# The down product of two FFN tiles by seven products instead of eight

## The chip, the cores and the metric

The kernel runs on one core of a Trainium2 chip. Four engines matter: TensorE (in the profile PE, its weight loads PEld), VectorE (DVE), ScalarE (ACT) and GpSimd (POOL); transfers are issued by SyncE (SP). The metric is the device time of one execution in microseconds, smaller is better. The kernel before was timed three times: 2411.37, 2413.34 and 2414.25 us, median 2413.34.

## The reference

A transformer block in fp32 over x of 2048 rows and 576 columns: attention with 32 heads of 18 that share one key and one value head, then a gated FFN without nonlinearity and with 4608 hidden columns. Cut to what matters here:

```python
h  = x + attention(layernorm(x))
n  = layernorm(h)
g  = n @ w_gate          # (2048, 576) @ (576, 4608)
u  = n @ w_up
h2 = h + (g * u) @ w_down   # (2048, 4608) @ (4608, 576): the down product
```

## The kernel before, in words

Rows are handled in four blocks b of 512 (TB). To keep fp32 accuracy with the faster fp32r matmuls, each operand is split into a high part (a cast to fp32r) and a low part (the rest, a subtraction on VectorE); a product is then three matmuls: high by high, high by low, low by high. `split` does the two steps. During the FFN the cast (`self.cast`) is on ScalarE for activations, on GpSimd for weights.

Attention of a block runs in pairs: `pair` issues the scores of two heads (two matmuls into one of two PSUM buffers named s) and the exp on ScalarE (P<-s); `flush` issues the matmuls of P by the values (acc). Attention of later blocks is woven into the FFN of an earlier block: `ffn(b)` issues one pair at every fourth step as long as `self.more(b + 2)` holds.

`ffn(b)` loops over 36 tiles f of 128 hidden columns. A tile has 27 steps of two matmuls, one for the gate (pg) and one for up (pu). Beside attention pg and pu lie in the two banks of tag f; without attention they are the halves of one of the two s buffers (gu). After the steps: `act.copy(g, pg)`, hf = pu * g on VectorE, the split of hf (ha, hl), the values of the pending pairs, and one piece of other work (`run_aux`: normalising heads, transposing a chunk, the output projection yo of the next block).

The down product is issued once per three tiles (CF = 3), after the first tile of the next three: eight groups (four row groups by two column halves of 288), each of nine matmuls (three tiles by three parts) into one PSUM bank, and an addition of the bank to h on VectorE. Banks go round over three, two of tag f and one of tag m (`ps_y`). In the loop:

```python
if k == 0 and todo:
    drain(self.down(b, *todo))
```

Weights come by DMA: `load_w` (wr, gate and up of one tile) and `load_wd` (wdr, one tile of w_down). `split_w` casts and splits the next tile's gate and up weights at step 3 (ws); `split_wd` does the same for w_down at steps 12 and 15 (wds). At a block's end the transposes of the normalised rows of the next block (`spread`, tx, X) alternate with the groups of the last down product.

The order on each engine is written by hand: it is the order in which the Python code issues instructions (`manual_schedule`). Tiles bring the semaphores for true dependences and for the reuse of buffers. A later instruction on an engine does not pass an earlier one.

The chunks of attention output go through oT, a buffer of nine times 512 columns; `transposed`, `chunk_of` and `project` use it.

## Time and profile before

| what | value |
|---|---|
| median of three runs | 2413.34 us |
| the profiled execution | 2414.04 us |
| its span, first to last instruction | 2412.3 us |
| granted TensorE clock, mean | 0.993 |
| TensorE busy | 2357.6 us, 98% |
| VectorE busy | 999.1 us, 41% |
| ScalarE busy | 1235.2 us, 51% |
| GpSimd busy | 357.9 us, 15% |

A row of the page or of an answer names line, engine, operation and tile (out<-in), then shape and count. In groups there follow the busy time, the mean of one in ns, the idle time ahead of it and what ended that; in a timeline a row begins with start and length in us, and the bracket at the end has the idle time before and its cause; the chain of waits in order of time has start, length and what was at work. Rows by tile give least, middle and greatest length in ns. Stretches (from:to) have length, TensorE's busy time, the granted clock PEclk, the share of the DMA engines and GB/s.

### The profile page before, as it was taken

What the parts mean: (1) busy time and instruction counts of PE and PEld (TensorE: products, weight loads), DVE (VectorE), ACT (ScalarE), POOL (GpSimd) and SP (SyncE); (2) the same over time, 40 slices, a digit from 0 to 9 for tenths busy, and PEclk for the clock granted to TensorE, in tenths of its full rate; (3) what the DMA queues carried; (4) which work ended last, traced back from release to release, by engine and by line L of the source; (5) the groups of instructions that cost most, each with busy time, mean ns of one, the idle gap of its engine ahead of it and who ended that gap; (6) DMA issues with size and microseconds to landing.
All of it is one profiled execution on the core that took longest, in us unless ns stands there. A gap on an engine that the chain in (4) does not pass through costs nothing.

```text
span 2412.3 us, 44160 instructions
## 1 busy us (share of the span) xinstructions
PE 2357.6 (98%) x18833; PEld 1658.7 (69%) x18833; DVE 999.1 (41%) x1719; ACT 1235.2 (51%) x1381; POOL 357.9 (15%) x406
## 2 busy tenths in 40 slices
PE   5999989999999999999999999999999999999999
PEld 4434434676776677777766767776777688888888
DVE  7323334343333345333333344433333364555454
ACT  4877867656555655555565556456555501111111
POOL 3000000111111111111111111111111112222221
PEclk9999999999999999999999999999999999999999
DMA  4212231222122221521222122322212222422321
GB/s 138 85 60 73 69 105 44 73 77 76 59 67 68 72 63 63 151 67 45 77 68 68 59 76 67 112 95 73 69 58 65 65 70 98 144 95 98 99 89 60
DMA packets 69298, 190.54 MB, mean 79 GB/s; under 512 B 8328, under 2 KB 9096, under 8 KB 69096
## 3 DMA queue, kind: packets, MB, share of 16 engines
q1 hardware_dynamic: 69096, 187.66, 24.6%
q8 instruction: 149, 2.44, 0.4%
q14 instruction: 53, 0.43, 0.1%
HBM read 159.39 MB, written 19.40 MB: 74 GB/s over the span
## 4 chain that ended last, share of the span: by engine, by line
PE 95%; DVE 2%; ACT 1%; issue 1%; DMA 1%; POOL 0%; SPq 0%; ACTq 0%; POOLq 0%; DVEq 0%
PE acc L503 19%; PE y L712 19%; PE pg L739 14%; PE gu L739 12%; PE s L498 12%; PE pu L739 11%; PE yo L608 3%; PE psq L335 2%; PE pt L541 1%; ACT P L499 1%; PE to L134 0%; PE tx L657 0%; DVE bsa L100 0%; PE psr L335 0%; DVE XT L86 0%
## 5 line engine op out<-in xcount | busy, mean ns | idle before, releaser
L499 ACT ACTIVATE P<-s 128x1024 f32<-128x1024 f32 x1024 | 1035.6, 1026 | 683.6 <-PE s L498 583.4
L739 PE MATMUL pg<-X,ws 64*128 64x512 f32 x2565 | 706.1, 392 | 0.0
L739 PE MATMUL pu<-X,ws 64*128 64x512 f32 x2565 | 705.7, 392 | 0.0
L739 PEld LDWEIGHTS pg<-X,ws 64*128 64x128 f32 x2565 | 474.4, 186 | 65.5 <-issue 6.1
L739 PEld LDWEIGHTS pu<-X,ws 64*128 64x128 f32 x2565 | 474.0, 186 | 40.3
L503 PE MATMUL acc<-P,V 128*32 128x512 f32 x4096 | 491.2, 599 | 2.6 <-DVE os L514 2.0
L712 PE MATMUL y<-wds,ha 128*128 128x288 f32 x2304 | 464.1, 296 | 2.5 <-ACT ha L85 1.2
L498 PE MATMUL s<-q,kT 56*128 56x512 f32 x2048 | 434.0, 421 | 12.9 <-DVEq L388 8.0
L712 PEld LDWEIGHTS y<-wds,ha 128*128 128x128 f32 x2304 | 368.4, 188 | 27.8 <-issue 25.2
L712 PE MATMUL y<-wds,hl 128*128 128x288 f32 x1152 | 340.0, 295 | 0.1
L498 PEld LDWEIGHTS s<-q,kT 56*128 56x128 f32 x2048 | 193.4, 185 | 208.3 <-ACT P L499 101.9
L85 POOL CAST ws<-wr 128x1152 fp32r<-128x1152 f32 x144 | 165.9, 1152 | 974.2 <-PE pu L739 414.2
L739 PE MATMUL gu<-X,ws 64*128 64x512 f32 x2646 | 307.2, 389 | 0.0
L503 PEld LDWEIGHTS acc<-P,V 128*32 128x32 f32 x4096 | 114.4, 109 | 250.4 <-issue 225.1
L739 PEld LDWEIGHTS gu<-X,ws 64*128 64x128 f32 x2646 | 247.3, 185 | 55.2 <-issue 4.2
L758 DVE TENSOR_TENSOR hf<-pu,g 128x512 f32<-128x512 f32 x95 | 65.7, 691 | 528.6 <-ACT g L754 528.6
L714 DVE TENSOR_TENSOR h<-h,y 128x288 f32<-128x288 f32 x384 | 172.7, 453 | 253.4 <-PE y L712 253.2
L754 ACT COPY g<-gu 128x512 f32<-128x512 f32 x49 | 28.8, 587 | 377.7 <-PE gu L739 377.7
L85 POOL CAST wds<-wdr 128x576 fp32r<-128x576 f32 x144 | 146.1, 1033 | 488.0 <-PE y L712 481.3
L712 PEld LDWEIGHTS y<-wds,hl 128*128 128x128 f32 x1152 | 216.1, 188 | 0.4 <-DVE hl L86 0.4
L86 DVE TENSOR_TENSOR ws<-wr,ws 128x1152 fp32r<-128x1152 f32 x144 | 204.4, 1420 | 0.0
L86 DVE TENSOR_TENSOR hl<-hf,ha 128x512 fp32r<-128x512 f32 x144 | 100.6, 699 | 151.3 <-ACT ha L85 151.3
(145 smaller groups left out, 1309.3 us busy)
## 6 DMA issues: line engine op xcount, KB each, us to landing
wr<-in_wgu_dram SPq DMA_DIRECT2D x144, 576.0 KB
wdr<-in_wd_dram SPq DMA_DIRECT2D x144, 288.0 KB
q<-q_dram SPq DMA_DIRECT2D x64, 216.0 KB
q_dram<-qs SPq DMA_DIRECT2D x16, 504.0 KB
X<-X SPq DMA_DIRECT2D x28, 256.0 KB
x<-in_x_dram SPq DMA_DIRECT2D x16, 288.0 KB
h<-in_x_dram SPq DMA_DIRECT2D x16, 288.0 KB
out_dram<-h SPq DMA_DIRECT2D x16, 288.0 KB
```

Of the source, the lines that this page charges most:

```text
L85: (copy or self.cast)(hi, src)
L86: self.dve.tensor_tensor(lo, src, f32(hi), ALU.subtract)
L335: pe.matmul(ps[:r], w[o:o + 64], m[o:o + 64], start=(k == 0), stop=(k == 13))
L498: self.pe.matmul(s_[:, i], self.kT[o:o + 56, t * P:(t + 1) * P], q[o:o + 56, pr], start=True, stop=True)
L499: self.act.activation(p_, s_, AF.Exp, scale=SCALE)
L503: self.pe.matmul(acc[32 * j:32 * j + 32, :], self.V[:, t, :], Ps[j // 2][:, j % 2, :], start=(t == 0), stop=(t == NT - 1), skip_group_chec ...
L608: pe.matmul(y[:, :HD], m, k, start=(i == 0), stop=(i == len(ms) - 1))
L712: pe.matmul(y[:, :HD], m, w, start=(i == 0), stop=(i == len(ms) - 1))
L714: dve.tensor_tensor(hs, hs, y[:, :HD], ALU.add)
L739: pe.matmul(ps, w[o:o + 64, wk, c], X[o:o + 64, xk, c], start=(j == 0), stop=(j == 26))
L754: act.copy(g, pg)
L758: dve.tensor_tensor(hf, pu, g, ALU.mult)
```

## The change

The down product is issued per pair of tiles. The left matrix (512 rows by 256 hidden columns) is seen as two by two blocks of 256 by 128, the right one (256 by 576) as two by two blocks of 128 by 288. Strassen's method in Winograd's form gives the four result blocks from seven products instead of eight, with four sums S of left blocks and four sums T of right blocks. Each product is three matmuls as before, for each of two row groups of 128: 14 stages of three matmuls per pair of tiles.

- `left`, after each odd tile: casts and subtractions for the plain left blocks that take part as they are (256 and 512 elements), the four sums S on VectorE, then the cast of S (1024 elements, ScalarE) and its subtraction. The tiles ha, hl go; A holds all parts.
- `sums_wd` and `split_wd`, at step 5 of each odd tile, on GpSimd: four sums T of 288 elements, then casts of 288, 576 and 1152.
- `rest_wd`, at step 12 of the next even tile, on VectorE: the three subtractions, and after them the loads of two further tiles of w_down.
- `down` runs the 14 stages over three banks in turn. A bank is read after each product and the next product is added to it in place, without starting at zero, so one product enters several results. Nine of the fourteen reads are additions on VectorE; five are copies on ScalarE into a small buffer (`tmp`), from which GpSimd adds to h.
- Place: after the even tile's steps, without attention ahead of that tile's g, with attention after its hf and the values.
- At a block's end `rest_wd` runs at step 18 of the last tile, ahead of `normal`.
- Room for A is taken from oT after block 0; attention output of later blocks goes through a buffer of one chunk (o_hl), and the fifth chunk is transposed after the fourth is projected. The buffer for raw wo goes from two to one.

```diff
-CF = 3
-NC = NF // CF
+NC = NF // 2
+HT = TB // 2
...
+    def sums_wd(self, n):
+
+        (b11, b12), (b21, b22) = (halves(self.wdr[i], HD) for i in (n, n + 1))
+        T = self.T
+        for i, (x, y) in enumerate(((b12, b11), (b22, T[:, 0]), (b22, b12), (b21, T[:, 1]))):
+            self.nc.gpsimd.tensor_tensor(T[:, i], x, y, ALU.subtract)
+
+    def wd_parts(self, n):
+        w = self.wds
+        return ((w[:, :, 0], self.wdr[n][:, 0:HD]), (w[:, :, 1:3], self.wdr[n + 1].rearrange("p (a d) -> p a d", a=2)),
+                (w[:, :, 3:7], self.T))
+
     def split_wd(self, n):
...
+        self.wds = self.wp.tile([P, 2, 7, HD], F32R, tag="wds", bufs=1, name=f"wds{n}")
+        for w, src in self.wd_parts(n):
+            self.nc.gpsimd.tensor_copy(w[:, 0], src)
+
+    def rest_wd(self, n):
+
+        for w, src in self.wd_parts(n):
+            self.dve.tensor_tensor(w[:, 1], src, f32(w[:, 0]), ALU.subtract)
+        for i in (n, n + 1):
+            del self.wdr[i]
+            self.load_wd(i + 2)
+
+    def left(self, hf):
+
+        dve, S, A = self.dve, self.S, self.A
+        (a11, a21), (a12, a22) = (halves(x, HT) for x in hf)
+        self.split(A[:, 0, 0], A[:, 1, 0], a11)
+        self.split(A[:, 0, 1:3], A[:, 1, 1:3], hf[1].rearrange("p (a q) -> p a q", a=2))
+        dve.tensor_tensor(S[:, 0], a21, a22, ALU.add)
+        dve.tensor_tensor(S[:, 1], S[:, 0], a11, ALU.subtract)
+        dve.tensor_tensor(S[:, 2], a11, a21, ALU.subtract)
+        dve.tensor_tensor(S[:, 3], a12, S[:, 1], ALU.subtract)
+        self.split(A[:, 0, 3:7], A[:, 1, 3:7], S)
+
+    def down(self, b, pair, W):
+
+        pe, dve, act, sp, pool = self.pe, self.dve, self.act, self.sp, self.nc.gpsimd
         h = self.h[b]
...
+        banks = [self.ps_f(f"y{b}_{pair}_0"), self.ps_f(f"y{b}_{pair}_1"), self.ps_m(f"y{b}_{pair}_2")]
+        for i, (t, bank, (x, w), first, (s, n), on_dve) in enumerate(STAGES):
+            y = banks[bank]
+            x_, w_ = ([o[:, k, j] for k in range(2)] for o, j in ((self.A, x), (W, w)))
+            ms = [(x_[k], w_[l]) for k, l in ((0, 0), (0, 1), (1, 0))]
+            for j, (m, k) in enumerate(ms):
+                pe.matmul(y[:, :HD], m[:, t * P:(t + 1) * P], k, start=(first and j == 0), stop=(j == 2), skip_group_check=True)
+            hs = h[:, t + 2 * s, n * HD:(n + 1) * HD]
+            if on_dve:
                 dve.tensor_tensor(hs, hs, y[:, :HD], ALU.add)
...
+            else:
+                z = self.tmp[:, self.n_tmp % 5]
+                self.n_tmp += 1
+                act.copy(z, y[:, :HD])
+                pool.tensor_tensor(hs, hs, z, ALU.add)
+            yield
+        if pair == NC - 1:
+            for s in (1, 3, 0, 2):
                 sp.dma_start(self.out[b * TB + s * P: b * TB + (s + 1) * P, :], h[:, s, :])
...
-                    if j == 12 and k == 1:
+                    if j == 5 and k:
+                        self.sums_wd(n_ - 1)
                         self.split_wd(n_ - 1)
-                    if j == 15 and k:
-                        self.split_wd(n_)
+                    if j == 12 and k == 0 and f:
+                        self.rest_wd(n_ - 2)
+                    if j == 18 and f == NF - 1:
+                        self.rest_wd(n_ - 1)
...
+            if todo and not on:
+                drain(self.down(b, *todo))
             g = self.hh.tile([P, TB], F32, tag="g", bufs=1, name=f"g{n_}")
             act.copy(g, pg)
...
-            self.split(a, l, hf)
-            hid.append((a, l))
+            hid.append(hf)
+            if k:
+                self.left(hid)
+                hid = []
             self.flush(len(self.pend))
+            if todo and on:
+                drain(self.down(b, *todo))
             if f < NF - 1:
                 self.run_aux()
...
+            todo = (f // 2, self.wds) if k else None
...
+P1, P2, P3, P4, P5, P6, P7 = (0, 0), (1, 1), (6, 2), (2, 6), (3, 3), (4, 4), (5, 5)
+
+
+STAGES = [(0, 0, P1, True, (0, 0), True), (1, 1, P1, True, (0, 0), True), (0, 2, P5, True, (1, 1), False),
+          (0, 0, P6, False, (0, 1), True), (1, 1, P6, False, (0, 1), False), (0, 2, P3, False, (0, 1), True),
+          (0, 0, P7, False, (1, 1), False), (1, 1, P7, False, (1, 1), True), (1, 2, P5, True, (1, 1), True),
+          (0, 0, P4, False, (1, 0), True), (1, 1, P4, False, (1, 0), False), (1, 2, P3, False, (0, 1), False),
+          (0, 0, P2, True, (0, 0), True), (1, 1, P2, True, (0, 0), True)]
```

A stage names the row group, the bank (0 and 1 of tag f, 2 of tag m), the pair of left and right parts, whether the bank starts at zero, the block of h, and whether VectorE reads.

More of the change, by code (lines that the diff above doesn't have):

```diff
@@ L532, in normalise @@
         del self.os[g]
-        for c in (g // 2,) * (g % 2) + (4,) * (g == NG - 1):
+        for c in (g // 2,) * (g % 2) + (4,) * (b == 0 and g == NG - 1):
             self.aux.append((self.round, lambda c=c: self.chunk(b, c), None))
@@ L614, in project @@
                     self.fill(2.4)
+        if c == 3 and b:
+            self.aux.append((self.round, lambda: self.chunk(b, 4), None))
         if c == 4:
@@ L690, in load_wd @@
             self.sp.dma_start(r, self.wd[n % NF])
-    def split_wd(self, n):
-        k = n % CF
-        if k == 0:
-            self.wds = self.wp.tile([P, 2, CF, D], F32R, tag="wds", bufs=1, name=f"wds{n}")
-        self.split(self.wds[:, 0, k], self.wds[:, 1, k], self.wdr.pop(n), self.nc.gpsimd.tensor_copy)
-        self.load_wd(n + 2)
-    def down(self, b, chunk, parts, wds):
-        pe, dve, sp = self.pe, self.dve, self.sp
-        h = self.h[b]
-        for s in range(NQ):
-            for n in range(2):
-                y = self.ps_y(2 * s + n, f"y{b}_{chunk}_{s}_{n}")
-                ms = []
-                for k, (a, l) in enumerate(parts):
-                    wh, wl = wds[:, 0, k, n * HD:(n + 1) * HD], wds[:, 1, k, n * HD:(n + 1) * HD]
-                    a_, l_ = a[:, s * P:(s + 1) * P], l[:, s * P:(s + 1) * P]
-                    ms += [(a_, wh), (a_, wl), (l_, wh)]
-                for i, (m, w) in enumerate(ms):
-                    pe.matmul(y[:, :HD], m, w, start=(i == 0), stop=(i == len(ms) - 1))
-                hs = h[:, s, n * HD:(n + 1) * HD]
-                dve.tensor_tensor(hs, hs, y[:, :HD], ALU.add)
-                yield
-            if chunk == NC - 1:
-                sp.dma_start(self.out[b * TB + s * P: b * TB + (s + 1) * P, :], h[:, s, :])
@@ L723, in ffn @@
             n_ = NF * b + f
-            k = f % CF
+            k = f % 2
             w = self.ws.pop(n_)
@@ L876, in run @@
             self.flush(len(self.pend))
+            del self.oT
+            self.room()
             for b in range(NB):
@@ L890, in both, with halves @@
         live = [x for x in live if next(x, drain) is not drain]
+def halves(ap, n):
+    return ap[:, 0:n], ap[:, n:2 * n]
 def f32(ap):
```

39 lines of the change are left out of this document (22 added, 17 removed).

## The prediction

> **What bounds the kernel now.** I read the page's totals and chain first, then the chain of waits over the last fifth in order of time, then timelines around single tiles. Lines of the page:
>
> ```profile
> span 2412.3 us, 44160 instructions
> PE 2357.6 (98%) x18833; PEld 1658.7 (69%) x18833; DVE 999.1 (41%) x1719; ACT 1235.2 (51%) x1381; POOL 357.9 (15%) x406
> ...
> PE 95%; DVE 2%; ACT 1%; issue 1%; DMA 1%; POOL 0%; SPq 0%; ACTq 0%; POOLq 0%; DVEq 0%
> ...
> L754 ACT COPY g<-gu 128x512 f32<-128x512 f32 x49 | 28.8, 587 | 377.7 <-PE gu L739 377.7
> ```
>
> TensorE carries 95% of the chain, so what it issues counts in full, and so does every wait put in front of it. The last row counts 49 FFN tiles whose sums lie in gu (no attention beside them); the other 95 of 144 have attention. With 36 tiles in each of four blocks, attention ends at tile 22 of block 2. Of the 72 new pair products, 45 then run beside attention (17, 17 and 11 in blocks 0, 1, 2), 23 without (6 and 17 in blocks 2, 3), three at block ends and one at the kernel's end.
>
> Rows of the chain of waits in order of time (start, us):
>
> ```profile
> 900.93 9.53 PE y L712 x72
> ...
> 2205.13 9.72 PE y L712 x72
> 2214.84 18.59 PE gu L739 x162
> ...
> 2384.68 12.49 PE gu L739 x108
> ...
> 2397.25 0.60 ACT g L754
> ...
> 2397.87 0.70 DVE hf L758
> ...
> 2398.60 0.63 ACT ha L85
> ...
> 2399.25 0.70 DVE hl L86
> ...
> 2408.77 0.46 DVE h L714
> ```
>
> One tile's gate and up take 18.59/3 = 6.20 us. Seventy-two down matmuls take 9.72 us, and 9.53 where they follow a projection's matmuls: 9.53/72 = 0.1323 each, and 0.19 to start. The rows from 2397.17 (2384.68 + 12.49) on show the chain that stands behind the last tile and is hidden behind others: g, product hf, cast, subtraction, 2.8 us until 2399.95.
>
> **The change part by part.**
>
> Matmuls. Per pair 14 x 3 = 42 replace 48; over 72 pairs 432 go: 432 x 0.1323 = -57.2 us. Products start 72 times for 48: 24 x 0.19 = +4.6.
>
> Reads. 14 rather than 5.3 a pair, over three banks in turn. The output projection already does this with groups of three matmuls and every read on VectorE (timeline):
>
> ```profile
> 1299.27 3.49 PE L608 MATMUL yo<-wos,oT 128*128 128x288 f32 x24
> 1299.97 3.29 DVE L609 TENSOR_TENSOR h<-h,yo 128x288 f32<-128x288 f32 x8 [0.85 <-PE yo L608]
> ```
>
> A group takes 3.49/8 = 0.44 us, a read 3.29/8 = 0.41. A stage of 0.397 us may wait for the read three stages back, which has 0.79 us; only nine of fourteen reads are VectorE's. I cost it at nothing (upper end 14 x (0.44 - 0.397) x 72 = +43). At the end of a product beside attention pu takes the bank of stage 13 and waits some 0.1 us: +4.5.
>
> What must stand before a product. This decides. `left` puts on VectorE, after each odd tile, four sums of 256 elements and subtractions of 256, 512 and 1024, and on ScalarE casts of the same sizes, the last of which needs all four sums. `rest_wd` puts subtractions of 288, 576 and 1152 behind them, after the subtraction for the next tile's gate and up weights. Product stage 2 needs the S of `left` and the T of `rest_wd`. Durations:
>
> ```profile
> L86 DVE TENSOR_TENSOR ws<-wr,ws x144: 1345/1353/1816, 406.9 to 2385.1; 128x1152 fp32r<-128x1152 f32 x144
> ...
> L85 POOL CAST wds<-wdr x144: 667/669/1796, 431.5 to 2390.7; 128x576 fp32r<-128x576 f32 x144
> L86 DVE TENSOR_TENSOR wds<-wdr,wds x144: 742/751/1215, 435.1 to 2393.7; 128x576 fp32r<-128x576 f32 x144
> ...
> L664 DVE TENSOR_TENSOR X<-tx,X 128x1024 fp32r<-128x1024 f32 x7 | 8.5, 1219 | 4.3 <-ACT X L666 4.3
> L666 ACT CAST X<-tx 128x1024 fp32r<-128x1024 f32 x7 | 6.8, 1026 | 0.3 <-PE tx L657 0.3
> L309 POOL TENSOR_TENSOR wq_l<-wqr,wq_h 128x630 fp32r<-128x630 f32 x3 | 4.5, 1504 | 0.2
> L309 POOL TENSOR_TENSOR wq_l<-wqr,wq_h 128x360 fp32r<-128x360 f32 x1 | 0.9, 879 | 0.1
> ```
>
> Between 576 and 1152 elements VectorE takes (1353-751)/576 = 1.045 ns an element, so 256 take 0.43 us and 288 0.45. ScalarE's 0.63 for 512 and 1.03 for 1024 give 0.43 for 256. GpSimd takes 2.3 ns an element between 360 and 630, so 288 take 0.71.
>
> Tiles without attention. Count from the end of an odd tile's gate and up matmuls. Product hf ends at 1.40 (rows at 2397); the cast of 512 at 2.06, its subtraction at 2.78 (the 256 piece, from the first tile, fits in that wait); four sums, 4.50; cast of 1024, 5.57; its subtraction, 6.83; weights 1152, 8.18; `rest_wd` 0.45 + 0.75 + 1.35, 10.73. TensorE has the next tile's 6.20 and stages 0 and 1 (0.79) to fill this: it arrives at 6.99. With the handover 10.8 is the lower end. GpSimd is still casting while VectorE forms the sums, and the two slow each other:
>
> ```profile
> 2214.91 2.40 POOL L85 CAST wds<-wdr 128x576 fp32r<-128x576 f32 x2 [8.56 <-PE y L712]
> 2215.25 1.53 DVE L86 TENSOR_TENSOR ws<-wr,ws 128x1152 fp32r<-128x1152 f32 x1
> 2216.71 1.88 DVE L86 TENSOR_TENSOR wds<-wdr,wds 128x576 fp32r<-128x576 f32 x2
> ```
>
> Two casts of 0.67 take 2.40; VectorE takes 1.53 + 1.88 for 1.35 + 1.50, 0.56 more. After a product GpSimd has a cast 1.15, sums 4 x 0.71, casts of 2016 elements some 2.3 and the next cast 1.15: about 7.5 us behind its last add, so 1 to 2 us of it meet the sums. I take 11.0, upper end 11.7. Stall 11.0 - 6.99 = 4.0; 23 x 4.0 = +92 (87 to 108). The down product's own cover is gone: before, it stood between a tile's chain and the next wait. The five adds (3.6 us) lie beside the product; the next weight cast behind them ends some 2 us into a tile of 6.20.
>
> The Trainium skill (SBUF — State Buffer, Who interferes with whom) says that VectorE with two SBUF inputs and a GpSimd read lock each other out, the later one for the whole instruction. The three rows agree in kind (2.40 for 1.34). By the full lock the stall would be some 2 us longer, +46 on the sum.
>
> The clock. Stretches of 3.41 us (us, PE busy, PEclk, DMA):
>
> ```profile
> 35.51:38.93 3.42, 2.15 (x10) 1.00 0.64 208
> ...
> 49.17:52.58 3.41, 0.46 (x2) 1.00 0.33 80
> 52.58:55.99 3.41, 2.25 (x14) 0.50 0.90 324
> ...
> 329.06:332.47 3.41, 1.48 (x12) 1.00 0.36 118
> 332.47:335.89 3.42, 0.00 (x0) 1.00 0.76 198
> ...
> 2407.78:2411.19 3.41, 0.96 (x8) 1.00 0.42 167
> 2411.00:2411.50 0.50, 0.00 (x0) 0.69 0.00 0
> ```
>
> After stretches with 0.46, 0.00 and 0.96 us of TensorE work the clock is half; after 1.48 and 2.15 it is not. The new gap is about 4.8 us with 0.8 us of work in it, so some stretches fall to 0.8 to 1.0. By where they can begin I estimate half of the pairs, each with one stretch or a little more at half speed, 1.9 us: 23 x 0.5 x 1.9 = +22 (0 to 23 x 3.4 = 78). The Trainium skill (TensorE: Matmul & The Clock Gate, What's actually happening) asks for a whole idle window of 3.4 us; the gap never has one, so by it this term is zero and the sum 22 less. The row at 2407.78 disagrees, with 0.96 us of work, so I keep the term.
>
> Tiles beside attention. Timeline there:
>
> ```profile
> 1503.91 1.02 ACT L499 ACTIVATE P<-s 128x1024 f32<-128x1024 f32 x1 [0.43 <-PE acc L503]
> ...
> 1504.83 0.61 ACT L85 CAST ha<-hf 128x512 fp32r<-128x512 f32 x1
> ...
> 1505.47 0.69 DVE L86 TENSOR_TENSOR hl<-hf,ha 128x512 fp32r<-128x512 f32 x1 [1.26 <-ACT ha L85]
> ...
> 1506.92 2.19 ACT L499 ACTIVATE P<-s 128x1024 f32<-128x1024 f32 x2 [1.49 <-PE s L498]
> ...
> 1507.37 0.19 PEld L498 LDWEIGHTS s<-q,kT 56*128 56x128 f32 x2
> ...
> 1508.53 0.19 PEld L498 LDWEIGHTS s<-q,kT 56*128 56x128 f32 x2
> ```
>
> Every answer of the trace shows ScalarE in the order of its queue, and there the cast of S now stands ahead of the next tile's exps: exp ends 1504.93, cast 256 1505.3, cast 512 1505.9, subtraction 1506.6, four sums 1508.2, cast of S 1509.3, first exp 1510.3. The third scores (1508.53) need the buffer that this exp empties: stall 1.8 us. ScalarE then keeps pace (1.02 an exp, scores each 1.16, from 1507.37 to 1508.53). `rest_wd`, 2.6 us after S, is no matter here: behind it lie most of a tile with scores and its values. In five cases, by the order in which the changed program issues, a projection (yo) follows an odd tile: its fourth group, due at 1507.5, needs a VectorE read that queues behind the subtraction of S (1510.5): some 3.4. Together 40 x 1.8 + 5 x 3.4 = +89 (0 to 100).
>
> Block ends and the last pair. Between a block's last tile and the next block's first, 13.0 us pass now (2067.12 - 2041.64 - 12.54):
>
> ```profile
> 2041.64 12.54 PE L739 MATMUL gu<-X,ws 64*128 64x512 f32 x108
> ...
> 2067.12 3.25 PE L739 MATMUL gu<-X,ws 64*128 64x512 f32 x26
> ```
>
> After, `rest_wd` of the last pair waits on GpSimd (adds until 0.8 us after the previous product, then 1.15 + 2.84 + 2.33: 7.1) and stands ahead of the normalisation (2.04) and of hf on VectorE: hf ends near 11.2, S near 16.6, twelve stages with X's subtractions between them near 24.4, so 18.2 after the tile's matmuls. With the 30 matmuls' 3.97 counted above: 3 x (5.2 + 3.97) = +27.6 (10 to 40). The end goes likewise from 15.1 (2412.3 - 2397.17) to some 19.3 us: without the normalisation hf ends near 9.1 and S near 14.5 after the previous product, twelve stages 19.3, so 13.1 behind the tile, then the read 0.46, the output 3.1 as now, and 2.6 because all four row blocks go out behind the last read: 4.2 + 3.97 = +8.2.
>
> Sum: -57.2 + 4.6 + 4.5 + 92 + 22 + 89 + 27.6 + 8.2 = +190.7. The profiled execution took 2414.04, 1.7 more than its span and 0.7 more than the median of the three; 2413.34 + 190.7 = 2604.
>
> **The rivals.**
>
> Faster: the matmuls removed are all that counts, because no chain ends last. -57.2 + 4.6 + 4.5 = -48, 2365 us. For it: 95% TensorE, 41% VectorE. Against it: the chain 10.8 must fall under 6.99. It decides only if the sums, casts and subtractions overlapped, and each needs the one before it. Chance 0.06.
>
> Attention hides its stall, because scores or values already issued cover the late exps: only +102, 2515. For it: ScalarE is 51% busy. Against: TensorE issues in order, and two s buffers are all. Chance 0.11.
>
> Sharing and clock worse: the full lock (+46) or most pairs at half clock (+30 or more): 2604 + 46 + some of the other, about 2660. For it: 2.40 us for 1.34. Against it: VectorE lost 0.56 us there, not all. Chance 0.11. No change to be measured: 0.01.
>
> **How the numbers follow.** The forecast, both chains uncovered, 2604, has 0.71, with its own range 2555 to 2640. The range 2505 to 2670 reaches the hidden attention stall and the worse sharing. About 0.2% tells from no change: faster 0.06, same 0.01, slower 0.93.
>
> **What would show it.** Right: y at about 5.8 us per 42 matmuls where nothing waits; without attention TensorE idle near 4 us in front of the third stage, released by VectorE's wds; a period near 22 us a pair where 28.31 x 2/3 = 18.9 stood; PEclk below 1.00 in some stretches after 1990; beside attention waits of the scores for ScalarE near 1.8 us, once a pair. Wrong: VectorE's wds subtraction ending before TensorE has finished the even tile; exps ahead of the cast of S; or gaps between stages 3 to 13 of one product, which would make the reads the cause.

## The result

The changed kernel takes 2653.24 us (median of four, 2648.9 to 2654.2), the kernel before 2412.49: a ratio of 1.0994, 95% interval 1.0975 to 1.1013. The prediction was 2604 us with a range of 2505 to 2670, slower with 0.93. So the sign was right and the time lies inside the range, 49 us above the forecast and 13 above the forecast's own range. The profiled execution has a span of 2651.8 us.

From the page of the changed kernel (busy time by engine, the shares of the chain that ended last), and then its longest waits of TensorE (engine and line, who ended the wait: us in total, times, longest):

```profile
PE 2426.8 (92%) x18401; PEld 1682.7 (63%) x18401; DVE 1384.6 (52%) x2415; ACT 1421.4 (54%) x1813; POOL 951.7 (36%) x1126
...
PE 64%; DVE 12%; ACT 6%; issue 4%; POOL 1%; DMA 0%; ACTq 0%; POOLq 0%; SPq 0%; DVEq 0%
```

```profile
PE y L749 <- DVE wds L722: 75.2, 41, 3.2
PE s L500 <- ACT P L501: 52.4, 47, 2.4
PE yo L615 <- DVE h L616: 20.3, 6, 5.3
...
PE tx L666 <- DVE xh L649: 13.6, 4, 5.0
```

TensorE issues 432 matmuls fewer and still has 69 us more of busy time (2426.8 for 2357.6); its share of the chain falls from 95% to 64%. The waits come in four kinds, and each is a place that the prediction named: the product for the down weights' subtraction, the scores for the exps, the output projection for VectorE, the next block's transposes for the normalised rows.

The same by stretch, of the kernel before and of the changed one. The columns are the stretch, its length, TensorE's busy time with its count, the granted clock, and DMA. The first row runs from the first gate and up matmul to the first tile without attention, the second from there to the end.

```profile
419.47:1918.42 1498.95, 1496.92 (x12307) 1.00 0.24 73
1918.42:2412.30 493.88, 484.57 (x3946) 0.99 0.29 94
```

```profile
418.91:2023.40 1604.49, 1523.74 (x12048) 0.98 0.22 68
2023.40:2651.80 628.40, 525.91 (x3769) 0.90 0.23 75
```

Beside attention 105.5 us are lost, without it 134.5.

**Without attention.** One pair of the changed kernel in order of time (start, us, engine, line, operation, tiles; in brackets the idle time before and what ended it):

```profile
2536.06 0.59 ACT L813 COPY g<-gu 128x512 f32<-128x512 f32 x1 [6.21 <-PE gu L793]
2536.64 1.16 POOL L717 CAST wds<-T 128x1152 fp32r<-128x1152 f32 x1
...
2537.29 2.33 DVE L88 TENSOR_TENSOR room<-hf,room 128x256 fp32r<-128x256 f32 x2
...
2537.74 1.34 POOL L87 CAST ws<-wr 128x1152 fp32r<-128x1152 f32 x1
2539.54 0.41 DVE L733 TENSOR_TENSOR S<-hf,hf 128x256 f32<-128x256 f32 x1
...
2541.12 1.05 ACT L87 CAST room<-S 128x1024 fp32r<-128x1024 f32 x1 [3.09 <-DVE S L736]
...
2543.34 1.35 DVE L88 TENSOR_TENSOR ws<-wr,ws 128x1152 fp32r<-128x1152 f32 x1
2544.61 1.12 DVE L722 TENSOR_TENSOR wds<-wdr,wds 128x288 fp32r<-128x288 f32 x2
...
2545.12 1.07 PE L749 MATMUL y<-wds,room 128*128 128x288 f32 x6 [2.65 <-DVE wds L722]
...
2545.65 1.35 DVE L722 TENSOR_TENSOR wds<-T,wds 128x1152 fp32r<-128x1152 f32 x1
...
2547.06 6.50 PE L749 MATMUL y<-wds,room 128*128 128x288 f32 x35 [0.87 <-DVE wds L722]
```

g starts right behind the odd tile's matmuls, and the last subtraction ends at 2547.00: 10.94 us, with the way from matmul to g the 11.0 of the prediction. TensorE waits 2.65 + 0.87 us. What the prediction did not have is that even the second matmul of the product waits: stage 0 needs the low half of the down weights too. And the 35 matmuls behind the wait take 6.50 us, where 35 at 0.1323 are 4.63. Three clock windows of 3.41 us around them, from the same trace and in the same columns as above:

```profile
2539.96:2543.37 3.41, 2.51 (x21) 1.00 0.00 0
2543.37:2546.79 3.42, 1.07 (x6) 1.00 0.31 65
2546.79:2550.20 3.41, 3.14 (x13) 0.50 0.73 281
```

A window with 1.07 us of TensorE work is followed by one at half clock, and in this stretch that happens in every pair, not in every second one. A pair takes 23.9 us where 18.9 stood.

**Beside attention.** The chain of waits of the changed kernel around the end of an odd tile (start, us, what):

```profile
1457.35 1.02 ACT P L501
1458.38 0.82 ACT room L87 x2
...
1461.04 0.35 DVE S L736
...
1462.37 1.03 ACT P L501
1463.44 0.50 PE s L500 x2
```

The exp that ends at 1463.40 is the first after the cast of S; ScalarE stood at that cast from 1459.20 on, and TensorE's next scores wait until 1463.44 for the buffer. In this stretch scores wait for exps 40 times, 49.6 us together (1.24 each; the prediction had 40 times 1.8), and the output projections 5 times, 14.9 us (17 forecast).

The clock falls here as well, which the prediction had no term for: 12 times, for 51.2 us together, the granted clock is half, and the mean of the stretch is 0.98. One case, a window of 3.41 us and what follows it, in the columns from above:

```profile
1492.08:1495.49 3.41, 1.53 (x13) 1.00 0.00 0
1495.49:1502.32 6.83, 5.80 (x25) 0.50 0.00 0
```

### The profile page after: what moved, and what is told of

The parts are those of the page before. It is cut to its first block, busy times and chain, and to the rows that moved or that the text cites. A ratio compares the mean times of both kernels' runs of the same rounds, so it can differ in the third digit from the quotient of the medians.

```text
span 2651.8 us, 45776 instructions
## 1 busy us (share of the span) xinstructions
PE 2426.8 (92%) x18401; PEld 1682.7 (63%) x18401; DVE 1384.6 (52%) x2415; ACT 1421.4 (54%) x1813; POOL 951.7 (36%) x1126
## 4 chain that ended last, share of the span: by engine, by line
PE 64%; DVE 12%; ACT 6%; issue 4%; POOL 1%; DMA 0%; ACTq 0%; POOLq 0%; SPq 0%; DVEq 0%
PE y L749 16%; PE pg L793 13%; PE acc L505 11%; PE s L500 8%; PE pu L793 7%; PE gu L793 6%; DVE room L88 3%; ACT P L501 3%; PE yo L615 3%; ACT room L87 2%; DVE wds L722 2%; DVE ws L88 1%; DVE S L734 1%; DVE S L733 1%; DVE S L736 1%
## 5 line engine op out<-in xcount | busy, mean ns | idle before, releaser
L757 POOL TENSOR_TENSOR h<-h,tmp 128x288 f32<-128x288 f32 x360 | 288.1, 809 | 1167.5 <-ACT tmp L756 1163.5
L749 PE MATMUL y<-wds,room 128*128 128x288 f32 x3024 | 494.6, 323 | 90.2 <-DVE wds L722 75.2
L749 PEld LDWEIGHTS y<-wds,room 128*128 128x128 f32 x3024 | 455.8, 207 | 159.0 <-DVE wds L722 85.9
L500 PE MATMUL s<-q,kT 56*128 56x512 f32 x2048 | 480.2, 427 | 62.6 <-ACT P L501 52.4
L752 DVE TENSOR_TENSOR h<-h,y 128x288 f32<-128x288 f32 x648 | 278.2, 453 | 263.3 <-PE y L749 255.8
L756 ACT COPY tmp<-y 128x288 f32<-128x288 f32 x360 | 143.7, 399 | 474.7 <-PE y L749 467.1
L500 PEld LDWEIGHTS s<-q,kT 56*128 56x128 f32 x2048 | 227.3, 186 | 266.7 <-ACT P L501 169.0
L706 POOL TENSOR_TENSOR T<-wdr,T 128x288 f32<-128x288 f32 x144 | 187.3, 1301 | 5.6
L87 ACT CAST room<-S 128x1024 fp32r<-128x1024 f32 x72 | 75.4, 1048 | 187.2 <-DVE S L736 187.2
L88 DVE TENSOR_TENSOR room<-hf,room 128x256 fp32r<-128x256 f32 (+1 forms) x144 | 109.3, 765 | 53.4 <-ACT room L87 49.3
```

The costliest lines, as they stand in the source:

```text
L87: (copy or self.cast)(hi, src)
L88: self.dve.tensor_tensor(lo, src, f32(hi), ALU.subtract)
L500: self.pe.matmul(s_[:, i], self.kT[o:o + 56, t * P:(t + 1) * P], q[o:o + 56, pr], start=True, stop=True)
L706: self.nc.gpsimd.tensor_tensor(T[:, i], x, y, ALU.subtract)
L749: pe.matmul(y[:, :HD], m[:, t * P:(t + 1) * P], k, start=(first and j == 0), stop=(j == 2), skip_group_check=True)
L752: dve.tensor_tensor(hs, hs, y[:, :HD], ALU.add)
```

## The experiments

Times are medians of four. The kernels with T formed once, with reads left out and with operands prepared once leave out part of the computation, so their result is not the block's; they serve for their time alone.

**The cast of S in the next even tile.** One edit, which moves the cast and the subtraction behind it:

```diff
-        self.split(A[:, 0, 3:7], A[:, 1, 3:7], S)
+    def left_s(self):
+
+        self.split(self.A[:, 0, 3:7], self.A[:, 1, 3:7], self.S)
...
+                    if j == 8 and k == 0 and f:
+                        self.left_s()
...
+                if f == NF - 1:
+                    self.left_s()
```

> One edit: the cast of S and the subtraction behind it are issued in the middle of the next even tile instead of at the end of the odd tile. My theory: beside attention the cast stands ahead of the next exps in ScalarE's queue and costs 1.7 us a pair; with it out of the way the 40 pairs beside attention lose this wait, 40 x 1.7 = -68 us, and the five projections behind an odd tile lose part of theirs. Without attention the weight subtraction of 1.4 us moves beside the cast, so the chain is some 1.06 us shorter, 23 x 1.06 = -24 us. Together 2653 - 92 = 2561 us, and the tiles beside attention go back to within 0.5 us of their length before. Rival: the wait beside attention comes from something else of the change (VectorE's four sums, the reads on ScalarE); then the tiles beside attention stay as they are, and the time is 2629 us or more. Second rival, for the tiles without attention alone: the period of a pair is held at seven clock windows of 3.413 us = 23.9 us; then a chain that is 1 us shorter buys nothing there, and the time is 2585 us.

2534.23 us, ratio to before 1.0496 (1.0479 to 1.0514): 119 us less than the change. The stretch beside attention falls from 1604.5 to 1526.7 (-78), the one without from 628.4 to 587.3 (-41). TensorE's longest waits in this kernel:

```profile
PE y L751 <- DVE wds L722: 51.1, 44, 2.0
...
PE yo L615 <- DVE h L616: 6.4, 6, 3.1
```

The wait of the scores for the exps falls from 52.4 us to 2.1, the projections' from 20.3 to 6.4. Beside attention the two together fall from 64.5 to 3.3 us, and the time at half clock from 51.2 to 23.9 us: some 61 us of waits and, at half of the time at half clock, some 14 us of clock are nearly all of the 78. So the cast in front of the exps was the price beside attention, where the prediction had it (89 us, all of it waits). The expected 92 for the whole edit was too little: without attention a chain 1 us shorter brought 1.75 us a pair (a pair takes 22.15). The trace says where the rest came from: every second product there now takes 9.0 us without any half clock, the others 10.45 with it. The rival of a period held at seven clock windows is out.

**Work for TensorE in the gap, first behind stages 0 and 1.**

```diff
+            if warm and i == 2:
+                a = self.ps_a(f"warm{b}_{pair}")
+                for j in range(12):
+                    pe.matmul(a, self.A[:, 0, 0, 0:P], self.X[:, 0, 0], start=(j == 0), stop=(j == 11))
...
-                drain(self.down(b, *todo))
+                drain(self.down(b, *todo, warm=True))
```

> Twelve matmuls of 128x512 with an unused result are put on TensorE ahead of the third stage of every pair product without attention (23 pairs), in the gap where TensorE otherwise waits 3.5 to 4 us. They take 12 x 0.23 = 2.8 us at full clock, less than the gap. My theory: the product's later stages take 6.5 us for 4.8 because the granted clock falls to 0.5 after a 3.41-us window with too little TensorE work; with work in the gap it stays at 1.00, the product takes 4.8, and 23 x 1.75 = 40 us go: 2613 us. Rival: the stages are slow because their reads, on three engines, hold the banks; then the product still takes 6.5 us and the time is 2653 us, or more by what the added work delays. Second rival: the added work takes its power or its ports from the chain, which then ends later: over 2653 us.

2671.67 us, ratio 1.1078 (1.1059 to 1.1096), slower than the change. The trace says why; timeline of TensorE, then two windows of it (here the pairs are time and count of PE, PEld, DVE, ACT and POOL, then the clock):

```profile
2527.03 1.57 PE L753 MATMUL y<-wds,room 128*128 128x288 f32 x5 [2.68 <-DVE wds L722]
...
2528.40 3.67 PE L749 MATMUL warm<-X,room 128*128 128x512 f32 x12
```

```profile
2523.95:2527.36 3.41, 0.73 (x4) 0.52 (x3) 3.24 (x4) 0.13 (x1) 0.00 (x0) 0.89 0.00 0
2527.36:2530.77 3.41, 3.41 (x12) 2.93 (x12) 2.28 (x4) 0.00 (x0) 0.00 (x0) 0.61 0.90 306
```

The work came behind the longer part of the gap: the clock had already been lost, and the work now stood in front of the product. The last subtraction ends at 2528.92, but the product's next matmul starts at 2531.91, behind the extra work; so the rival of a chain that itself ends later is out. It tests nothing but its place, so it was run again ahead of stage 0 (`if warm and i == 0`, all else alike):

> The twelve unused matmuls of 128x512 now stand ahead of the first stage of every pair product without attention (23 pairs), not ahead of the third, behind which only 0.9 us of the gap was left. They run while TensorE waits for the chain, 2.8 us of the 3.5. Theory (clock): no 3.41-us window has less than 2 us of TensorE work any more, the granted clock stays at 1.00, the twelve stages that took 6.5 us take 4.8, and 23 x 1.75 = 40 us go: 2613 us, a pair period near 22.1 us instead of 23.9. Rival (reads pace the late stages): period and time as they are, 2653 us.

2620.31 us, ratio 1.0858 (1.084 to 1.0876): 33 us less than the change, 32 of them without attention. The product of one pair, and the window that now has least work:

```profile
2493.00 5.20 PE L753 MATMUL y<-wds,room 128*128 128x288 f32 x35 [0.88 <-DVE wds L722]
```

```profile
2491.80:2495.20 3.40, 2.52 (x18) 1.00 0.93 329
```

The 35 matmuls take 5.20 us for 6.50 with the same reads, and a pair 22.6 us. The clock did that, not the reads on three engines. 33 us for the 40 expected: 5.20 is still more than 4.8.

**T formed once.** `sums_wd(0)` for the first pair, no T sums for the others:

```diff
-                        self.sums_wd(n_ - 1)
+                        if n_ == 1:
+                            self.sums_wd(0)
```

> The four sums of down weights (T) are formed for the first pair only, not for each of 72 pairs (so T, and the output with it, is that of the first pair); everything else stays, casts and subtractions of T too. My theory: GpSimd's T sums lie beside VectorE's first subtraction of a pair without attention, which takes 2.33 us for 1.1, and beside the four sums of S. Without them the chain there ends about 1.2 us earlier: 23 x 1.2 = -28 us, and the three block ends get some 2.8 us each back, -8: 2617 us. Rival: the sums only cost the 0.2 us that the prediction took for sharing: -5 and -8, 2640 us. Second rival: the period of a pair without attention is held at seven clock windows (23.9 us), and the shorter chain buys nothing there: 2645 us. Beside attention nothing changes by any of them.

2609.58 us (2608.36 to 2630.86), ratio 1.0843 (1.0797 to 1.0888): -44, of which 35 without attention and 11 beside it, where nothing was expected (mostly the two block ends). One pair's chain:

```profile
2450.20 0.59 ACT L814 COPY g<-gu 128x512 f32<-128x512 f32 x1 [6.24 <-PE gu L793]
...
2452.20 0.69 DVE L88 TENSOR_TENSOR room<-hf,room 128x512 fp32r<-128x512 f32 x1 [0.36 <-ACT room L87]
...
2458.92 1.35 DVE L722 TENSOR_TENSOR wds<-T,wds 128x1152 fp32r<-128x1152 f32 x1
```

From g to the end of the last subtraction it is 10.07 us, 0.87 less than in the change: without GpSimd beside it VectorE's subtractions of hf are as short as the prediction had them. Some 1.5 us a pair came of it, more than the chain got shorter. The rest is the clock, whose mean there rose from 0.90 to 0.94: of the sixteen steady pairs (2229 to 2570) 5 now have a product of about 9.3 us without any half clock, the others one of about 10.7 with it, where in the change every product has it.

**All fourteen reads on VectorE**, and in another kernel **five reads left out**:

```diff
-            if on_dve:
+            if True:
```

```diff
-            else:
-                z = self.tmp[:, self.n_tmp % 5]
-                self.n_tmp += 1
-                act.copy(z, y[:, :HD])
-                pool.tensor_tensor(hs, hs, z, ALU.add)
```

> All fourteen reads of a product are VectorE's; ScalarE's five reads and GpSimd's five adds are gone, the result is the same. Theory (the prediction's upper end for the reads): VectorE needs 14 x 0.45 us for a product that now takes 6.05 us beside attention, so the product becomes 6.4 to 6.7 us and the time 2653 + 72 x 0.35 to 0.65 = 2678 to 2700 us. Rival (the sharing is what costs): without GpSimd's adds VectorE's reads and sums are faster and the time falls below 2640 us. If the reads lie wholly beside the matmuls, it stays at 2653 us.

> The five reads of a product that ScalarE takes, and GpSimd's five adds, are left out (those parts of the sum are not added to h); VectorE's nine stay, the matmuls too. Theory: the product takes 6.05 us beside attention where 42 matmuls and a start are 5.75, because stages wait for a bank's read; with five reads fewer half of this goes, 72 x 0.15 = -11 us, and without attention GpSimd is free 1 us earlier for the weight casts, which its wait for the tile's weight buffer takes back: 2642 us. Rival (reads at nothing, as predicted): 2653 us. Second rival (ScalarE's reads behind late exps hold the banks): more than 0.3 us a product, under 2630 us.

2632.24 (ratio 1.0907, 1.0889 to 1.0925) and 2628.16 us (1.0885, 1.0867 to 1.0904): -21 and -25, both wholly beside attention (1582 us for 1604.5). In both, a product there still takes 6.03 to 6.09 us, so neither who reads nor five reads fewer moves its pace. The theory of the first (a longer product, 2678 to 2700 us) is wrong, and its time lies where its rival has it (below 2640); the second's time lies in the range of its second rival (under 2630), but not for that reason, since the product did not get shorter. The gain sits in two places by the starts of the products: near the output projections (1 to 3 us each) and at the ends of blocks 0 and 1, where from the product before the last to the last it is 15.4 and 16.6 us for 21.6 and 22.7 (half of that the next pair gives back). There the change's chain runs through GpSimd's adds, as the prediction had it; the chain at the end of block 0 in the changed kernel:

```profile
1004.95 0.54 POOL h L757
...
1008.45 3.33 POOL T L706 x3
...
1012.99 1.16 DVE wds L722
...
1015.95 1.96 DVE xh L649 x4
```

So the part of the change that gives five reads to ScalarE and GpSimd costs some 21 us: on VectorE all fourteen are cheaper.

**The product one pair later.** The product moves to the end of the next pair's odd tile, across block ends too; the core:

```diff
+                    if j == 5 and k == 0 and n_:
+                        self.sums_wd(n_ - 2)
+                        self.split_wd(n_ - 2)
+                    if j == 8 and k == 0 and n_:
+                        self.left_s()
+                    if j == 8 and k and n_ > 1:
+                        self.rest_wd(n_ - 3)
...
+            if k and self.todo and not on and not last:
+                drain(self.down(*self.todo))
...
+            if k:
+                self.left(hid)
+                hid = []
+                self.todo = b, f // 2
```

> The whole computation, with the order changed: the product of a pair is issued at the end of the next pair's odd tile, behind 12.4 us of gate and up instead of 6.2, also across block ends; T's sums, the casts and the cast of S are issued in the next even tile, the weight subtractions in the next odd tile. My theory: all that costs time in the changed kernel is the chain that stands before a product, and the matmuls removed are worth 57 us. Then 2413 - 57 + 5 (starts) + 5 (third bank) + 8 (end of the kernel) = 2374 us, with 2365 to 2400 for what is left at block ends. If VectorE's or GpSimd's load itself is the price (sharing, 14 reads), TensorE still waits 1 us or more per pair: over 2420 us.

2634.47 us, ratio 1.0914 (1.0896 to 1.0932). Without attention the product now waits for nothing, but gate and up do. One even tile there:

```profile
2466.86 0.99 POOL L706 TENSOR_TENSOR T<-wdr 128x288 f32<-128x288 f32 x1
...
2468.32 1.03 DVE L733 TENSOR_TENSOR S<-hf,hf 128x256 f32<-128x256 f32 x1
...
2471.74 1.81 DVE L88 TENSOR_TENSOR ws<-wr,ws 128x1152 fp32r<-128x1152 f32 x1
...
2473.61 4.61 PE L796 MATMUL gu<-X,ws 64*128 64x512 f32 x38 [1.81 <-DVE ws L88]
```

Sums of 0.41 us take 1.03 beside GpSimd's, and the next tile's weights come 1.81 us late. Beside attention the cast of S again stands ahead of exps, now behind VectorE's slowed sums (up to 4 us a pair against the next version: 3.9 in block 0, some 1.5 in block 1). My theory that only the chain in front of the product counts is wrong: VectorE beside GpSimd is the next bound.

**Later, and GpSimd kept off VectorE.** The sums of S behind the next weight subtraction; beside attention T's sums, the casts and the cast of S in the odd tile; without it ScalarE casts the weights:

```diff
+                        self.split_w(n_ + 1, None if on else self.cast)
+                    if j == 5 and k == 0 and n_:
+                        self.early = not on
+                        self.sums()
+                        if self.early:
+                            self.sums_wd(n_ - 2)
+                            self.left_s()
+                            self.split_wd(n_ - 2, self.cast)
+                    if j == 4 and k and n_ > 1 and not self.early:
+                        self.sums_wd(n_ - 3)
+                        self.left_s()
+                        self.split_wd(n_ - 3)
```

> The product one pair later as before, with GpSimd kept away from VectorE: the four sums of S come behind the next weight subtraction; beside attention T's sums, the weight casts and the cast of S are issued in the odd tile, where VectorE and GpSimd stood idle; without attention ScalarE, which is idle there, casts the weights in GpSimd's place. Theory: VectorE's slowdown beside GpSimd (0.92 to 1.03 us for sums of 0.42, 2.2 us for subtractions of 1.1) and the cast ahead of the exps are all that kept the later product from its gain. Then a pair beside attention takes 0.4 us less than two thirds of three tiles before, 45 x 0.4 = -18, a pair without it 18.6 us for 18.9, 23 x 0.3 = -7, and the end of the kernel costs 8: 2396 us (2385 to 2425). If VectorE's own load is the price, it stays over 2450 us.

2490.54 us, ratio 1.0319 (1.0301 to 1.0336): 144 less, and not the 2396 hoped for. Beside attention it works; here are twelve pairs of block 1 as one stretch (time and count of PE, PEld, DVE, ACT, POOL, then the clock):

```profile
1081.08:1464.01 382.93, 382.45 (x3085) 268.57 (x3081) 216.78 (x376) 251.52 (x316) 157.85 (x172) 1.00 0.21 65
```

TensorE has nothing to wait for, and yet 382.93/12 = 31.9 us a pair is what two thirds of three tiles took before (nine groups from 1088.67 to 1518.23, 31.8). With every wait gone the smaller count of matmuls did not show. Without attention a pair takes 20.5 us.

**Operands prepared once.** That made the gain itself the question:

```diff
-                        self.sums_wd(n_ - 1)
-                        self.split_wd(n_ - 1)
+                        if n_ == 1:
+                            self.sums_wd(n_ - 1)
+                            self.split_wd(n_ - 1)
...
-        for w, src in self.wd_parts(n):
+        for w, src in self.wd_parts(n) if n == 0 else ():
...
-                self.left(hid)
+                if n_ == 1:
+                    self.left(hid)
```

> The operands of the pair products are prepared for the first pair only: S, T, their casts and subtractions, and those of hidden values and down weights, are left out for the other 71 pairs (their products use the first pair's operands); matmuls, reads and loads stay. So no chain stands before a product, and what is left is the gain of the smaller count of matmuls. By the prediction's own terms 2413 - 57.2 + 4.6 + 4.5 = 2365 us. Theory by the products as measured: one takes 6.04 us where two thirds of one of three tiles took 9.79 x 2/3 = 6.53, so 72 x 0.49 = 35 us, 2378 us, less a shorter chain at block ends and at the end, some 10 to 20 us: 2360 to 2370. Rival (the reads or the three banks hold TensorE even without the chain): above 2400 us.

2398.39 us, ratio 0.994 (0.9923 to 0.9957), above the expected 2360 to 2370 and next to the rival's 2400. Without any chain the change is worth 15 us, not 48. The same kernel with all fourteen reads left out too:

```diff
-            if on_dve:
-                dve.tensor_tensor(hs, hs, y[:, :HD], ALU.add)
-            else:
...
-                act.copy(z, y[:, :HD])
-                pool.tensor_tensor(hs, hs, z, ALU.add)
```

> As the run with operands prepared once (2398 us), and all fourteen reads of every product left out too (nothing is added to h), so no stage and no tile behind a product waits for a read. Theory: the product's 6.04 us (5.75 for 42 matmuls and a start) come from its groups of three matmuls, not from the reads, as the run with nine reads kept the length; it stays at 5.95 to 6.05. What the reads do cost is the tile behind a product beside attention: its up matmul waits for the bank of the last stage, the gate matmul runs alone, and the tile takes some 0.3 us longer; 45 x 0.3 = -13 us: 2385 us, nearly all of it beside attention. Rival A (the reads pace the product): the product falls to 5.75 us and the time to 2398 - 72 x 0.29 - 13 = 2364 us. Rival B (neither): 2398 us, and the missing gain beside attention lies elsewhere.

2356.22 us, ratio 0.9768 (0.9752 to 0.9785). The reads cost 42 us. The two stretches, first with reads, then without, and below them the start of a tile behind a product, in the same order:

```profile
419.07:1916.93 1497.86, 1490.24 (x12048) 1.00 0.23 73
1916.93:2395.70 478.77, 468.67 (x3769) 1.00 0.29 98
```

```profile
418.88:1887.74 1468.86, 1464.52 (x12048) 1.00 0.23 75
1887.74:2354.70 466.96, 463.01 (x3769) 1.00 0.29 99
```

```profile
1193.07 0.45 PE L793 MATMUL pg<-X,ws 64*128 64x512 f32 x1
1193.35 0.49 PE L793 MATMUL pu<-X,ws 64*128 64x512 f32 x1
```

```profile
1207.55 0.40 PE L785 MATMUL pg<-X,ws 64*128 64x512 f32 x1
1207.55 0.62 PE L785 MATMUL pu<-X,ws 64*128 64x512 f32 x2
```

29 of the 42 us lie beside attention, 45 products: 0.64 us each as a mean, in which two block ends with 1.9 us each are counted. A pair of block 1 goes from 30.94 to 30.36 us or from 30.14 to 29.56, 0.58 us, and the trace divides it. 0.2 us are the product's (6.04 to 5.85 us). 0.37 us are the tile's right behind it: 8.70 us with reads, 8.33 without, where the odd tile takes 8.33 to 8.34 in both kernels. With reads its first gate matmul runs alone, because its up matmul starts 0.28 us later, when its bank has been read; without them the two run together from the start. Where transposes stand between the product and that tile, it takes 8.33 us with reads too. So the bank of the last read costs more than the reads do within the product. Without attention, where gate and up have banks of their own, a pair goes from 18.44 to 18.26 us, the product's share alone; the rest of the 12 us there is the end of the kernel (12.7 to 7.0 us from the last gate and up matmul on) and the block end (11.2 to 9.3). My theory (the groups of three set the pace) is wrong, rival A is nearest in time (2364 us), with a product of 5.85 us for its 5.75.

**Three at once:** late cast, work ahead of stage 0, all reads on VectorE.

> Three edits at once on the changed kernel: the cast of S in the next even tile (alone -119 us), the unused matmuls ahead of the first stage (alone -33), all fourteen reads on VectorE (alone -21). If the three causes are separate, they add up: 2653 - 173 = 2480 us. My theory: nearly so, but the late cast already made the gap without attention 1 us shorter and with it the fall of the clock rarer, and both the late cast and VectorE's reads help the same output projections, so some 15 us are counted twice: 2495 us. Rival (one of them only uncovers the next wait): over 2520 us.

2511.2 us, ratio 1.0406 (1.0389 to 1.0423), 16 us more than the expected 2495: -142 for the sum of -173. Beside attention -81 us for -103, so the two other edits added only some 3 us to the late cast's 78, and VectorE's reads helped where the late cast helps as well; without it -61 for -76.

**The later product with three more moves** (the casts behind g on ScalarE, GpSimd for the odd tile's weights, T earlier at block ends):

```diff
+                    if j == 1 and k and n_ > 1 and self.early < 2:
+                        if not self.early:
+                            self.sums_wd(n_ - 3)
+                        self.left_s()
+                        self.split_wd(n_ - 3, None if on else self.cast)
+                    if j == 3:
+                        self.split_w(n_ + 1, None if on or k else self.cast)
...
+                        self.early = 2 if on and f == NF - 2 else 0 if on else 1
```

> The later product again, with three more moves: without attention the cast of S and the weight casts stand on ScalarE behind the even tile's g, and GpSimd casts the odd tile's gate and up weights; at the end of a block beside attention T's sums and casts come in the even tile, so that GpSimd is free for the copies of the normalised rows. Theory: a pair without attention goes from 20.5 to 18.7 us (23 x 1.8 = -41), the two block ends get some 4 us each back (-8): 2490 - 49 = 2441 us. Rival (VectorE's load with GpSimd beside it is the price there, whatever the order): 2470 us or more. By either it stays above 2413 us, since a product one pair later saves only 0.5 us against three tiles' products and lengthens block ends and the end of the kernel.

2469.12 us, ratio 1.0226 (1.0209 to 1.0243), for 2441 expected and 2470 or more by the rival. A pair without attention takes 19.1 us (18.7 expected), and its product waits only this much:

```profile
2407.39 5.20 PE L756 MATMUL y<-wds,room 128*128 128x288 f32 x35 [0.26 <-DVE wds L722]
```

The stretch without attention is 521.5 us (551.9 in the version before), the one beside it 1531.4 (1517.5): the move at block ends lost 14 us, and no better place was tried. Neither version beats the kernel before; with the operands free altogether only 15 us are to be had.

## Why the prediction was right, and where its sum was off

Three differences of runs on the chip add up to the change: 2411.9 to 2356.2 (no chain, no reads), to 2398.4 (with reads), to 2653.2 (with chains). The cut between the last two is not quite sharp, since chains that the kernel before had too, at block ends and the end, are missing in the first two. From the last gate and up matmul to the end of the kernel it is 15.1 us before, 20.2 in the change, 12.7 with operands prepared once and 7.0 without reads; the first gap at a block end is 12.6, 18.9, 11.0 and 9.1 us in the same order. And the reads are priced where no chain stands beside them: the 21 us that the change saves with all reads on VectorE lie in the rows of the chains.

| part of the sum | predicted, us | measured, us |
|---|---|---|
| matmuls removed and starts | -52.6 | -55.7 |
| reads, and the bank of stage 13 | +4.5 | +42.2 |
| chains beside attention, two block ends among them | +107.4 | +106.6 |
| chains without, clock, one block end, the end | +131.4 | +149.6 |
| sum | +190.7 | +242.7 |

(The last two rows are stretches of traces, 1604.5 - 1497.9 and 628.4 - 478.8, the others medians, so that the column does not come out at 2653.2 - 2411.9 = 241.3 exactly.)

Matmuls: right in size. Some 4 of the 55.7 us are not theirs, though, but the shorter end of the kernel without chains; and a steady pair without attention saves 0.61 us (18.26 for 18.87), where the sum has 0.73 for a pair.

Reads: the step that failed. "I cost it at nothing (upper end ... +43)", and 42 were measured. The prediction quoted the row nearest to the new form, the output projection's groups of three at 0.44 us, and then reckoned with the room that a read has on average. Its +4.5 for pu was the right place at a fraction of the size: 0.1 us a pair, where the tile behind the product took 0.37 us longer beside attention, and the product itself 0.2. That the upper end of +43 meets the 42 is luck: it stands for products 0.6 us longer. Which reads hold the product itself stayed open, since leaving out ScalarE's five did not shorten it.

Tiles without attention: 11.0 forecast, 10.94 from g on measured, but by terms that make up for each other. Consecutive operations of VectorE overlapped by some 0.1 us, and sharing with GpSimd was put at 0.2 us where the run without T's sums took 0.87 off the chain. The Trainium skill (SBUF — State Buffer, Who interferes with whom) would have VectorE and GpSimd lock each other out, some 2 us longer by the prediction's estimate. In the changed kernel it was less than that, 0.87 us; little of GpSimd's work meets the chain there. The later product's trace fits the lock: VectorE's sums of 0.41 us took 0.92 to 1.03 beside GpSimd's, and they ended 0.28 us behind the end of GpSimd's sum of the time (at 2469.35, 2470.30 and 2471.25 for 2469.07, 2470.02 and 2470.97).

The clock: right in kind, too small. 33 us by the run with work in the gap, for 22; it falls in every pair of the steady stretch, for which the prediction had half of them. The Trainium skill (TensorE: Matmul & The Clock Gate, What's actually happening) asks for a whole idle window. The trace does not need one: the window at 2543.37 has 1.07 us of work and the next has half clock. Beside attention the sum has no clock at all, and 51.2 us of that stretch ran at half clock.

Tiles beside attention: right in place and in number, 40 waits of scores and 5 of projections, but each was shorter: 64.5 us of waits for 89. Moving the cast was worth 78 us, some 14 of them by the clock. That the row comes out at 106.6 for 107.4 is partly luck: smaller waits, a clock that the sum has not, and block ends a little longer than forecast. The rival that attention hides its stall is out.

Block ends and the last pair: right in mechanism, the chain at 1004.95 is the forecast one. The gap at the end of block 0 is 18.9 us (1012.71 to 1031.66), for 18.2, at the ends of blocks 1 and 2 it is 20.1 and 20.0, and the end of the kernel takes 20.2 for 19.3. Of the 18 us too many without attention some 11 are the clock. For the other 7 no run was made, but the trace places most of them: around the last output projection, in that stretch (2037.54 to 2077.98), the changed kernel takes 40.4 us where the one with operands prepared once takes 27.2. That is 13.3 more, and a steady pair has only 5.5 more; TensorE waits 5.35 us there for VectorE's h, and the prediction had no term for it.

The rival of sharing and clock both worse (2660) has the nearest time, but not for its reasons alone: most of what it needed came from the reads.

## What to carry to other kernels

Ahead of trading matmuls for preparation, ask what stands between the last input and the first use: here 57 us of matmuls were bought with chains worth 255. Then price every smaller group with its read by the nearest row of the same form, the one with a read behind each group, and follow the bank of the last group into the work that comes next. And an operation put on a quiet engine costs what is queued behind it, not its own duration: one cast of 1 us ahead of exps cost 78.

## What the runs showed of the hardware

- 1.07 us of TensorE work in a window of 3.41 us was followed by half clock (2543.37), and so were 1.53 us (1492.08); 2.51 and 2.52 us were not. But neither were 1.48 us in the kernel before (the window at 329.06), so the work within the window alone does not tell.
- VectorE's sum of 256 elements took 0.41 us alone and 0.92 to 1.03 beside GpSimd's sums in the later product, ending 0.28 us behind one of them; its subtraction of 1152 took 1.35 and 1.81. Four sums took 3.50 us there (2468.32 to 2471.82) for 1.54 in the change (2539.54 to 2541.08), and the weights behind them came 1.81 us late, with VectorE busy for 60% of the span and GpSimd for 41%.
- A gate matmul whose up partner came 0.28 us later ran alone, and the tile took 8.70 us; where both banks were free the two, on half the rows each, started together, and it took 8.33.
